# A hand-ordered kernel for a state-space scan and dilated attention: its issue order rearranged, with the load of the B matrices moved, mask constants moved on GpSimd, and four state reloads on ScalarE

## The chip, the cores and the metric

The kernel runs on one core of a Trainium2 chip. The metric is the device time of one launch in microseconds (us), the median of several runs. The five engines of the core appear under the profile's names: PE (TensorE, the matrix engine; PEld is its weight load), DVE (VectorE), ACT (ScalarE), POOL (GpSimd) and SP (SyncE, which here only issues DMA transfers; SPq in the profile). Each engine works through its own instructions in the order in which the program has them, and waits at one until what it needs is there. PSUM is the memory into which TensorE's matmuls write; VectorE and ScalarE copy ("cast") results from there into the on-chip SBUF.

## The reference

Two independent parts read a sequence of 2048 tokens with 448 channels each, and their outputs stand side by side.

```python
# part A: a diagonal state-space layer
dt = exp(log_dt); Lam_bar = exp(dt * Lam)            # complex, 448 states
B_bar = ((Lam_bar - 1.0) / Lam)[:, None] * Bmat
Bu = einsum("bld,pd->blp", x, B_bar)
for t in range(L):
    h = Lam_bar * h + Bu[:, t, :]                    # a scan over 2048 tokens
y = 2.0 * einsum("blp,dp->bld", hs, Cmat).real + x * Dskip
# part B: dilated sliding attention, 16 heads of 28, window 8, dilation 2
q, k, v = split(x @ wqkv)
logits[s, w] = q[s] . k[s - 2*w] * scale             # masked where s - 2*w < 0
o[s] = sum_w softmax(logits)[s, w] * v[s - 2*w]
out = o @ wo
return concatenate([a, b], axis=-1)
```

## The kernel before, in words

The 2048 tokens are laid out as 128 chunks of 16 consecutive tokens; "token j" below is the j-th of every chunk, so one tile of 128 rows holds token j of all chunks.

**Part B.** x of token j is loaded by a transposing DMA (L363, four tiles of 128x128 each; L359, L366 and L367 fetch the rest of the channels). TensorE projects Q and K (L478, L511 with all 128 rows; L485 two at a time with 64 rows each, for the remaining 64 channels of two tokens; for these the 64 rows are first copied to the other half of the partitions, "the dup copy"). Results leave PSUM by casts (helper L215 and L217 on ScalarE, L219 and L221 on VectorE). VectorE multiplies q with shifted k (L651, L653, L657, the products), TensorE sums each product over the 28 channels of a head in 32 columns (L669, L675, the logits) and adds the mask (L287), VectorE takes the maximum (L698), TensorE subtracts it (L702, "sub"), ScalarE exponentiates (L708), VectorE divides (L717, L719), a transposing DMA turns the weights (L724). V is projected at L750 and L757. VectorE makes the weighted sum of V, four groups g of four tokens (g = 3 and 2 first, then 1 and 0), each a run of multiplications L814 and additions L817 that ends with L826, or with L829 for g = 0. Groups 3, 2 and 1 are transposed by a DMA (L852), group 0 by TensorE (L864, tile pt_o). TensorE multiplies with wo (L880, L888, L895), and L905 sends the rows out. There are 4 staging rows for them.

**Part A.** GpSimd and VectorE work out the powers of Lam_bar from the parameters (GpSimd at L1056 to L1075; then ScalarE's exponential and sine, L1079 and L1082; then GpSimd again, L1106 to L1121; VectorE builds Gd at L1127 and the power matrices pw at L1179). TensorE forms the input matrix Bcat from Gd and B (L1163, tile ps_b, with B in the tile ra: loaded at L954 and L955, 784 KB, half of it copied to other partitions by the "ra copy"). The scan goes by seven groups m of 64 states (a complex state takes two rows): local matmuls on x (L1229, L1238), then a chain that TensorE and ScalarE hand back and forth (L1248 to L1300: casts e, eA, eB, eight small steps ubuf, S), and at its end the states of the inner tokens. There a "reload" puts an earlier result, already cast to SBUF, back into a PSUM tile, so that matmuls can add to it: either ScalarE copies it (L1304) or TensorE multiplies it with the identity (L1306). The output y is 15 matmuls per token over the states and x (L1428, L1432); L1447 sends it out from 8 staging rows. Six PSUM banks serve everything, with one double tile beside them.

**The order.** The program first collects 685 units of work (`Planner.add`), each with its possible engines. `Planner.run` then issues them in the order of the table `ORDER` (L48 on): an entry modulo 1000 is the unit's number, and an entry over 1000 picks the second of the unit's engines. Since each engine is an in-order queue, the table alone sets what stands ahead of what on every engine, SP's queue of DMA transfers among them. All units of a PSUM tile take the next free bank in that order. Where TensorE goes from one shape of tile to another (128 rows, pairs of 64 rows, logits in 32 columns) the planner reckoned with an extra cost when the table was made; the table itself is only a list.

Of the kernel before, what the change touches and what calls it, by code (L numbers as in the profile page):

```python
# [45 lines left out]
YG = ((3,), (7,), (11,), (1, 5), (9,), (0, 4), (8,), (2, 6), (10,), (12, 13), (14,), (15,))  # L46
YSPLIT = 8
ORDER = [  # L48
    1, 22, 4, 5, 2, 3, 0, 36, 7, 38, 39, 24, 1037, 26, 28, 30, 8, 6, 40, 9, 41, 42, 19, 13, 12, 49, 1043, 11,
    10, 1045, 44, 50, 62, 63, 64, 1066, 21, 220, 29, 51, 53, 65, 52, 31, 32, 54, 55, 1058, 56, 59, 1057, 60, 61,  # L50
    69, 70, 1046, 71, 72, 1073, 74, 75, 67, 87, 76, 1068, 171, 78, 79, 80, 81, 1077, 172, 82, 83, 103, 104, 88,
    1047, 105, 107, 106, 84, 86, 14, 95, 96, 85, 97, 98, 1154, 174, 15, 33, 167, 99, 90, 91, 92, 260, 168, 221,
    157, 158, 93, 373, 1094, 181, 18, 108, 109, 16, 17, 155, 48, 165, 110, 111, 1166, 100, 131, 112, 113, 182,
    175, 115, 116, 173, 183, 1114, 101, 176, 1102, 119, 134, 20, 135, 141, 137, 156, 161, 162, 159, 160, 117,
    118, 120, 163, 505, 164, 506, 507, 121, 89, 188, 508, 35, 139, 136, 123, 124, 125, 122, 127, 495, 509, 184,
    496, 179, 147, 143, 185, 126, 189, 490, 510, 511, 491, 492, 493, 494, 138, 144, 513, 514, 186, 512, 498,
    128, 499, 140, 129, 180, 177, 133, 497, 187, 132, 130, 196, 178, 500, 520, 485, 486, 206, 207, 501, 503,
    529, 487, 521, 502, 504, 522, 208, 209, 148, 145, 515, 531, 516, 517, 150, 518, 519, 149, 146, 261, 190,
    523, 142, 191, 197, 202, 203, 151, 488, 222, 223, 525, 169, 524, 192, 193, 224, 227, 225, 229, 228, 226,
    230, 194, 231, 232, 195, 233, 234, 527, 489, 262, 235, 236, 263, 237, 23, 238, 239, 210, 264, 240, 241, 266,  # L60
    242, 268, 265, 204, 25, 243, 244, 267, 270, 245, 246, 247, 269, 1250, 198, 200, 271, 272, 248, 249, 526,
    253, 1254, 211, 27, 205, 299, 199, 201, 213, 214, 530, 251, 252, 273, 274, 170, 255, 257, 300, 256, 258,
    259, 275, 276, 215, 216, 301, 302, 305, 303, 277, 306, 338, 339, 340, 278, 279, 341, 34, 280, 281, 307, 212,
    343, 342, 282, 345, 533, 534, 304, 283, 344, 347, 535, 346, 348, 308, 284, 152, 153, 536, 285, 541, 309,
    310, 349, 350, 286, 287, 311, 312, 351, 352, 289, 288, 290, 313, 353, 354, 314, 412, 355, 292, 293, 356,
    315, 316, 294, 291, 295, 317, 357, 296, 318, 319, 358, 359, 320, 617, 360, 217, 218, 297, 298, 449, 219,
    321, 322, 361, 362, 374, 363, 364, 323, 324, 375, 325, 326, 366, 365, 367, 369, 327, 368, 376, 1328, 537,
    370, 379, 380, 371, 372, 377, 329, 413, 330, 381, 414, 415, 378, 382, 383, 384, 1331, 333, 416, 417, 419,
    528, 418, 1332, 334, 385, 421, 386, 336, 420, 422, 564, 565, 423, 424, 538, 539, 540, 568, 335, 387, 388,
    337, 425, 426, 566, 450, 389, 390, 427, 428, 569, 451, 391, 429, 392, 430, 452, 393, 394, 431, 432, 453,  # L70
    567, 455, 395, 396, 433, 434, 454, 457, 456, 435, 436, 397, 398, 458, 571, 459, 542, 460, 399, 400, 437,
    443, 461, 401, 462, 463, 438, 439, 402, 464, 465, 403, 404, 466, 467, 624, 468, 1440, 441, 469, 442, 625,
    470, 445, 471, 444, 446, 447, 570, 472, 473, 629, 572, 630, 474, 634, 475, 476, 477, 1405, 637, 478, 638,
    479, 480, 482, 573, 448, 626, 574, 575, 576, 532, 631, 632, 577, 627, 407, 481, 483, 578, 579, 619, 620,
    484, 409, 628, 621, 622, 639, 635, 636, 557, 640, 641, 550, 543, 633, 544, 545, 551, 552, 553, 554, 643,
    644, 406, 642, 408, 410, 558, 559, 547, 561, 662, 665, 666, 623, 560, 546, 616, 667, 580, 671, 672, 663,
    664, 668, 669, 555, 556, 670, 645, 673, 657, 658, 659, 648, 651, 652, 411, 646, 618, 649, 650, 562, 563,
    679, 548, 549, 602, 609, 610, 611, 653, 654, 612, 603, 604, 655, 606, 656, 613, 674, 675, 614, 615, 607,
    647, 676, 586, 608, 660, 661, 605, 587, 581, 582, 591, 592, 677, 588, 589, 583, 590, 678, 593, 594, 595,
    596, 680, 681, 597, 682, 598, 599, 584, 585, 683, 684, 600, 601]  # L80
TWO_PI = 2.0 * math.pi
MAGIC = 12582912.0

# [1485 lines left out]
```

## Time and profile before

| what | us |
|---|---|
| runs: median (lowest to highest of 3) | 139.23 (138.53 to 139.27) |
| the profiled execution: its own time | 138.77 |
| its span on the profile; time outside the span | 137.1; 1.67 |
| TensorE busy in the span | 130.2 (95%) |
| VectorE busy | 121.8 (89%) |
| ScalarE busy | 94.1 (69%) |
| GpSimd busy | 20.9 (15%) |

The profiled execution lies 0.46 us below the median of the runs. TensorE ran at the full granted clock in every stretch of the span. Busy time of TensorE contains short waits: a matmul's recorded duration (0.38 us for 512 columns) is longer than its distance to the next one in a running series (0.22 us), so up to 0.16 us of waiting behind one shows as busy.

### The profile page before, as it was taken

Reading aid. Unit: us, or ns where it says so; the run is one execution under the profiler, and the core shown is the slowest. Engines: PE = TensorE matmul, PEld = TensorE weight load, DVE = VectorE, ACT = ScalarE, POOL = GpSimd, SP = SyncE. Lnnn points to the kernel's source line nnn. Section 1 sums busy time; section 2 is a strip of 40 time slices with the busy share of each in tenths; the row PEclk is TensorE's granted clock in tenths of the full one; section 3 lists DMA queues with packets and bytes.
Section 4 is the critical chain, followed back from the end, with each engine's and each line's share of the span. In section 5 each row is a group of like instructions: output and inputs, shape, how many; then the busy total and the mean of one; then the engine's idle time right before and its main releaser. Section 6 shows DMA issues by size and latency. Waiting matters only on the chain.

```text
span 137.1 us, 2829 instructions
## 1 busy us (share of the span) xinstructions
PE 130.2 (95%) x1059; PEld 66.2 (48%) x1064; DVE 121.8 (89%) x131; ACT 94.1 (69%) x209; POOL 20.9 (15%) x69
## 2 busy tenths in 40 slices
PE   7999969999999899999999999999999999999990
PEld 2533424464555363556345643455664555545750
DVE  1636789999999999999999999999999999999950
ACT  3359949899493767588789799979659332608641
POOL 7581898009100000000000000000000000000000
PEclk9999999999999999999999999999999999999999
DMA  4978953564452444478948329810074434824443
GB/s 132 270 125 206 183 89 37 107 180 87 76 115 53 88 83 108 124 217 169 144 75 163 73 45 241 196 33 2 0 134 138 133 103 91 219 61 133 135 154 114
DMA packets 41694, 16.58 MB, mean 121 GB/s; under 512 B 33685, under 2 KB 41044, under 8 KB 41681
## 3 DMA queue, kind: packets, MB, share of 16 engines
q1 hardware_dynamic: 41618, 16.40, 52.2%
q8 instruction: 8, 0.13, 0.4%
q14 instruction: 5, 0.04, 0.1%
q10 hardware_dynamic: 63, 0.01, 0.0%
HBM read 4.32 MB, written 3.67 MB: 58 GB/s over the span
## 4 chain that ended last, share of the span: by engine, by line
PE 60%; DVE 19%; SPq 10%; ACT 4%; DMA 3%; issue 2%; DVEq 0%; ACTq 0%
PE y_ps L1432 15%; DVE prods L653 7%; SPq L363 7%; PE scb L1229 6%; PE wo_ps L888 5%; PE scp L1229 5%; DVE prods L657 3%; DMA rb<-in_B_x_dram 3%; DVE pw L1179 3%; DVE prods L651 2%; PE logits L669 2%; PE wo_ps L895 2%; PE scb L1283 2%; PE scP L1229 2%; PE v_ps L757 2%
## 5 line engine op out<-in xcount | busy, mean ns | idle before, releaser
L814 DVE TENSOR_TENSOR prods<-attn,vd 128x3584 bf16<-128x3584 bf16 x12 | 23.9, 2017 | 0.0
L817 DVE TENSOR_TENSOR rb<-rb,prods 128x3584 bf16<-128x3584 bf16 x11 | 22.2, 2018 | 0.1
L653 DVE TENSOR_TENSOR prods<-qk 128x3072 bf16<-128x3072 bf16 (+1 forms) x15 | 19.2, 1323 | 0.2
L478 PE MATMUL qk_ps<-rb 128*128 128x512 bf16 x60 | 14.6, 379 | 1.3 <-DMA rb<-in_B_x_dram 1.3
L1432 PE MATMUL y_ps<-Ccat,qk 128*128 128x448 bf16 x60 | 14.5, 352 | 0.0
L215 ACT CAST qk<-wo_ps 128x448 bf16<-128x448 f32 (+1 forms) x16 | 8.3, 533 | 7.1 <-PE wo_ps L888 4.8
L215 ACT CAST vd<-v_ps 128x448 bf16<-128x448 f32 x16 | 8.3, 534 | 4.3 <-PE logits L287 2.1
L1229 PE MATMUL scb<-xaT_sb,Bcat 128*128 128x512 bf16 x42 | 11.1, 381 | 0.1
L1229 PEld LDWEIGHTS <-Bcat 128*128 128x128 bf16 x84 | 7.7, 100 | 7.1 <-issue 0.8
L217 ACT ACTIVATE qk<-qk_ps 128x512 bf16<-128x512 f32 (+1 forms) x17 | 9.8, 598 | 1.8 <-PE qk_ps L485 1.7
L1432 PE MATMUL y_ps<-Ccat,h 128*128 128x448 bf16 x45 | 11.0, 353 | 0.0
L757 PE MATMUL v_ps<-rb 128*128 128x448 bf16 x48 | 10.3, 354 | 0.0
L478 PEld LDWEIGHTS <-rb 128*128 128x128 bf16 x60 | 5.4, 97 | 8.5 <-issue 2.1
L1276 ACT CAST ubuf<-scb 128x64 bf16<-128x64 f32 x35 | 6.7, 217 | 3.8 <-PE scb L1283 1.8
L215 ACT CAST qk<-qk_ps 128x512 bf16<-128x512 f32 (+2 forms) x14 | 8.2, 587 | 1.3 <-POOL angr L1073 1.0
L657 DVE TENSOR_TENSOR prods<-qk 128x768 bf16<-128x768 bf16 (+3 forms) x18 | 9.1, 563 | 0.0
L215 ACT CAST qk<-y_ps 128x448 bf16<-128x448 f32 (+1 forms) x9 | 5.8, 678 | 4.8 <-PE y_ps L1432 4.8
L1432 PEld LDWEIGHTS <-qk 128*128 128x128 bf16 x60 | 5.9, 98 | 5.2
L814 DVE TENSOR_TENSOR rb<-attn,vd 128x3584 bf16<-128x3584 bf16 x4 | 8.1, 2024 | 0.2
L1179 DVE TENSOR_TENSOR pw<-Dm,spair 128x1920 bf16<-128x1920 bf16 x7 | 8.2, 1192 | 0.0
L1229 PE MATMUL scp<-xaT_sb,Bcat 128*128 128x512 bf16 x30 | 7.9, 382 | 0.0
L888 PE MATMUL wo_ps<-wo_p,rb 128*128 128x448 bf16 x36 | 7.8, 353 | 0.1
(200 smaller groups left out, 258.6 us busy)
## 6 DMA issues: line engine op xcount, KB each, us to landing
out_dram<-qk SPq DMA_DIRECT2D x32, 112.0 KB, 1.7
vd<-vd SPq DMA_DIRECT2D x3, 392.0 KB, 4.4
rb<-in_B_wqkv_dram SPq DMA_DIRECT2D x3, 336.0 KB, 4.2
qk<-in_A_x_dram SPq DMA_DIRECT2D x1, 448.0 KB
ra<-in_A_B_re_dram SPq DMA_DIRECT2D x1, 392.0 KB, 4.3
ra<-in_A_B_im_dram SPq DMA_DIRECT2D x1, 392.0 KB
rb<-in_A_C_re_dram SPq DMA_DIRECT2D x4, 98.0 KB, 2.8
rb<-in_A_C_im_dram SPq DMA_DIRECT2D x4, 98.0 KB, 4.3
```

The source lines that it names most:

```text
L215: nc.scalar.copy(out, in_)
L217: nc.scalar.mul(out, in_, scale)
L478: nc.tensor.matmul(out(n), lhsT=w(n, full, k), rhs=self.xT[:, j:j + 4, k, :], start=(not rfirst and k == 1), stop=(rfirst and k == KT - 1) ...
L653: V.tensor_tensor(out.rearrange("p i j k q -> p i (j k) q"), qq.unsqueeze(1).to_broadcast([NCH, 2, 4 * nk, NCH]), bass.AP(kk.tensor, kk.of ...
L657: V.tensor_tensor(jk(out[:, i, a:e]), qq, kk, op=ALU.mult)
L757: nc.tensor.matmul(box["ps"][:].rearrange("p h d -> p (h d)"), lhsT=self.xT[:, j, k, :], rhs=self.wv[:, k, :], start=False, stop=(k == KT ...
L814: V.tensor_tensor(tmp[i].rearrange("p (j d h) -> p j d h", j=8, d=DH), aa, self.vd[:, o:o + 8], op=ALU.mult)
L817: V.tensor_tensor(acc, acc, tmp[i], op=ALU.add)
L888: nc.tensor.matmul(ps[:], lhsT=self.oTd[g][:, a + kt], rhs=self.wo_p[:, 5 * e + kt, :], start=False, stop=(kt == 2), skip_group_check=True)
L1179: V.tensor_tensor(t[:], self.o["Dm"][:].rearrange("p (a b) -> p a b", b=2).unsqueeze(1).to_broadcast([NCH, 2 * NPW, 32, 2]), self.sp[:, m ...
L1229: mt(box[i], lhsT=self.Bcat[:, k, m, :], rhs=self.xk(slice(i, None, 4), k), start=(i % 2 == 0 and k == 0), stop=False, **kw)
L1432: nc.tensor.matmul(ps, lhsT=h, rhs=self.Ccat[:, m, :], start=(m == 0 and not skip), stop=(m == NM - 1), skip_group_check=True)
```

## The change

Only the table `ORDER` is another: the same 685 units, in a new order, some on their other engine. Two lines of each table as an illustration:

```diff
 ORDER = [
-    1, 22, 4, 5, 2, 3, 0, 36, 7, 38, 39, 24, 1037, 26, 28, 30, 8, 6, 40, 9, 41, 42, 19, 13, 12, 49, 1043, 11,
-    10, 1045, 44, 50, 62, 63, 64, 1066, 21, 220, 29, 51, 53, 65, 52, 31, 32, 54, 55, 1058, 56, 59, 1057, 60, 61,
+    1, 22, 4, 5, 2, 3, 0, 36, 7, 1037, 38, 39, 40, 24, 26, 28, 41, 8, 6, 9, 30, 49, 1043, 44, 50, 62, 1042, 13,
+    63, 45, 64, 1065, 51, 1052, 54, 55, 56, 21, 29, 53, 69, 70, 58, 1057, 1059, 1060, 1061, 46, 74, 1066, 71,
...
```

SP's queue near the start, as a difference; each row is one issue or a run of equal ones (`x4`), with the line, the tile written and the source:

```order
 L340 DMA rb<-in_B_wqkv_dram 128x3x448
 L342 DMA rb<-in_B_wqkv_dram 64x448
-L363 DMA_TRANSPOSE rb<-in_B_x_dram 128x4x128 x4
+L363 DMA_TRANSPOSE rb<-in_B_x_dram 128x4x128 x8
 L954 DMA ra<-in_A_B_re_dram 64x7x448
 L955 DMA ra<-in_A_B_im_dram 64x7x448
-L363 DMA_TRANSPOSE rb<-in_B_x_dram 128x4x128 x4
 L359 DMA_TRANSPOSE xb_rest<-in_B_x_dram 128x1x128
 L363 DMA_TRANSPOSE rb<-in_B_x_dram 128x4x128 x2
```

The first four transposes are x of tokens 8 to 11, the next four x of tokens 4 to 7. The two loads of B stood between them and now stand behind both.

VectorE's queue from its first work on x to Gd, before:

```order
L219 COPY rb<-rb 64x4x128
L221 TENSOR_SCALAR qk<-qk_ps 128x4x128
L219 CAST qk<-qk_ps 64x4x128
L219 CAST qk<-qk_ps 128x4x128
L219 COPY rb<-rb 64x4x128
L219 CAST qk<-qk_ps 128x4x128
L221 TENSOR_SCALAR qk<-qk_ps 128x4x128
L651 TENSOR_TENSOR prods<-qk 128x1536
L219 CAST qk<-qk_ps 128x4x128
L651 TENSOR_TENSOR prods<-qk 128x1536
L219 COPY rb<-rb 64x4x128
L219 COPY ra<-ra 128x7x64
```

Behind these stand one more product L651, Gd (L1127) and three powers (L1179). And now:

```order
L219 COPY wm<-rb 128x512
L221 TENSOR_SCALAR qk<-qk_ps 128x4x128
L219 CAST qk<-qk_ps 128x4x128 x2
L219 CAST qk<-qk_ps 64x4x126
L221 TENSOR_SCALAR qk<-qk_ps 64x512 x2
L221 TENSOR_SCALAR qk<-qk_ps 128x4x128
L219 CAST qk<-qk_ps 128x4x128 x3
L574 COPY qk<-qk 128x24
L651 TENSOR_TENSOR prods<-qk 128x1536 x2
L221 TENSOR_SCALAR qk<-qk_ps 64x512 x2
L651 TENSOR_TENSOR prods<-qk 128x1536
L1127 TENSOR_TENSOR Gd<-Dm,gs 128x896
```

Twelve casts out of PSUM (the rows with qk_ps, counting `x2` and `x3`; the first is the L221) stand ahead of Gd instead of six, the ra copy follows Gd instead of preceding it, and the dup copies of x (rb<-rb 64x4x128) have gone to ScalarE. After Gd VectorE has four such casts fewer than before. The first TensorE work on tokens 4 to 7 is now a 64-row pair (L485), which needs the dup copy; before it was a 128-row unit (L478), which doesn't.

GpSimd's queue around the second half of the parameters, as a difference (mrow and mcol are the mask constants that L287 reads):

```order
 L1074 TENSOR_SCALAR kc<-kf 128x105
 L1075 TENSOR_TENSOR angr<-angr,kc 128x105
+L272 MEMSET mrow 128x4
+L274 AFFINE_SELECT mrow<-mrow 128x2x2
+L276 MEMSET mcol 128x512
+L280 AFFINE_SELECT mcol<-mcol 128x128 x4
 L1106 TENSOR_TENSOR cs<-sh 128x210
 L1107 TENSOR_SCALAR cs<-cs 128x210
```

The masks stood behind L1121, the last step of the parameters, and now stand in the gap in which ScalarE works out the sine. The clearing of S (L1194) went the other way, from ahead of L1056 to behind L1121.

SP's queue in the last third, from the Dskip row on (L852 are the transposes of groups g = 2 and g = 1, L905 outputs of part B, L1447 of part A):

```order
L1399 DMA rb<-in_A_Dskip_dram 128x448
L905 DMA out_dram<-qk 128x448 x2
L770 DMA vd<-vd 112x1792
L771 DMA vd<-vd 15x1792
L852 DMA_TRANSPOSE rb<-rb 128x14x128 x2
L1447 DMA out_dram<-qk 128x448 x4
L905 DMA out_dram<-qk 128x448
```

Thirty of the 32 outputs now stand behind the transpose of g = 1. Before, ten outputs stood ahead of it and 22 behind.

Elsewhere the order moves in many places. Reloads by ScalarE (L1304) go from seven to four, by TensorE (L1306) from nine to twelve. Changes of tile shape on TensorE go from 51 to 58, three of the seven before the first local matmuls of the scan and four behind, where the logits of the first eight tokens come in four blocks between the scan's steps instead of two. Counting PSUM casts and copies together, VectorE has one more than before and ScalarE one fewer (its reloads aside).

## The prediction before the run

> **What bounds the kernel now.** I read the shares of the engines first, then stretches of the span, then the waits that TensorE has in them. In the first row each engine has busy us, share and instructions; in the stretches the columns are length, busy time of PE, PEld, DVE, ACT and POOL, then clock and DMA.
>
> ```profile
> PE 130.2 (95%) x1059; PEld 66.2 (48%) x1064; DVE 121.8 (89%) x131; ACT 94.1 (69%) x209; POOL 20.9 (15%) x69
> ```
>
> ```profile
> 17.26:24.00 6.74, 5.41 (x32) 2.16 (x32) 6.24 (x8) 4.94 (x10) 6.15 (x8) 1.00 0.41 63
> 24.00:52.00 28.00, 27.45 (x314) 14.21 (x313) 27.63 (x39) 20.75 (x38) 3.75 (x6) 1.00 0.46 98
> 52.00:75.00 23.00, 22.77 (x215) 11.58 (x216) 22.61 (x19) 18.26 (x52) 0.00 (x0) 1.00 0.69 143
> 75.00:109.00 34.00, 33.59 (x254) 18.11 (x256) 33.73 (x21) 27.78 (x73) 0.00 (x0) 1.00 0.42 98
> 109.00:133.66 24.66, 24.61 (x171) 13.66 (x169) 22.59 (x17) 10.85 (x21) 0.00 (x0) 1.00 0.45 132
> 133.66:137.10 3.44, 0.00 (x1) 0.00 (x0) 0.00 (x0) 0.53 (x1) 0.00 (x0) 1.00 0.35 111
> ```
>
> TensorE is 95% busy. Length less PE busy gives its idle time by stage: 1.33 from 17.26 to 24, 0.55 from 24 to 52, 0.23, 0.41 and 0.05 in the three stages of scan and output, 3.44 at the end. VectorE is as full from 24 to 109 (27.63 of 28.00, 22.61 of 23.00, 33.73 of 34.00). So a change gains only where TensorE waits, and what it adds to TensorE costs in full. The two large waits by name:
>
> ```profile
> 18.59 1.46 PE L478 MATMUL qk_ps<-rb 128*128 128x512 bf16 x6 [1.33 <-DMA rb<-in_B_x_dram]
> ...
> 45.57 0.59 PE L702 MATMUL logits<-mx,nident 128*128 128x512 bf16 x2 [0.55 <-DVE mx L698]
> ```
>
> At 18.59 TensorE has waited 1.33 for x of tokens 4 to 7; at 45.57 it has waited 0.55 for VectorE's maximum. Short waits hide as busy, since a matmul's record is longer than its distance to the next one:
>
> ```profile
> 109.08 0.38 PE L1306 MATMUL scp<-qk,ident 128*128 128x512 bf16 x1
> 109.51 0.73 PE L888 MATMUL wo_ps<-wo_p,rb 128*128 128x448 bf16 x3
> ```
>
> One reload holds 109.08 to 109.51. A running series gives 0.22 per 512 columns (step 2), so about 0.2 of the 0.43 is waiting, and no idle time shows. Counted so over all starts after 52 us (columns, shape changes and small steps allowed for), I get some 2.9 us of waits, 0.69 of them visible as idle above. That is all that the scan and the output could give back.
>
> The sum is made against the profiled execution, 138.77 us (span 137.10 and 1.67 outside it); the median of the runs is 0.46 above. A measurement of this kernel tells about 0.5%, 0.70 us, from no change: faster is below 138.53, slower above 139.93.
>
> **Step 1: B behind x of tokens 4 to 7, and what is late next.**
>
> ```profile
> 9.24 0.67 SPq L954 DMA_DIRECT2D ra<-in_A_B_re_dram  x1
> ...
> 10.37 1.42 DVE L219 CAST qk<-qk_ps 64x512 bf16<-64x512 f32 x2 [0.46 <-PE qk_ps L478]
> 10.63 5.24 SPq L363 DMA_TRANSPOSE rb<-in_B_x_dram  x4
> ...
> 18.54 0.29 DVE L219 COPY rb<-rb 64x512 bf16<-64x512 bf16 x1 [0.47 <-DMA rb<-in_B_x_dram]
> 18.86 0.64 DVE L219 COPY ra<-ra 128x448 bf16<-128x448 bf16 x1
> 19.42 0.94 DVE L651 TENSOR_TENSOR prods<-qk 128x1536 bf16<-128x1536 bf16 x1
> ...
> 20.28 0.73 DVE L1127 TENSOR_TENSOR Gd<-Dm,gs 128x896 bf16<-128x896 bf16 x1
> ...
> 22.04 0.39 PE L1163 MATMUL ps_b<-Gd,ra 128*128 128x128 bf16 x4
> ```
>
> ```profile
> 14.61 3.74 DMA rb<-in_B_x_dram
> ...
> 21.01 3.52 DVE pw L1179 x3
> ```
>
> ```profile
> out_dram<-qk SPq DMA_DIRECT2D x32, 112.0 KB, 1.7
> ...
> ra<-in_A_B_re_dram SPq DMA_DIRECT2D x1, 392.0 KB, 4.3
> ```
>
> ```profile
> DMA to landing us min/median/max: 2.8/3.9/4.2
> ```
>
> (The rows at 14.61 and 21.01 are the chain's; then come two DMA issues, with KB and us to landing, and the landing times of x.) SP's two issues for B take 10.63 - 9.24 = 1.39 us, so the four transposes now issue from 9.24 on and the last lands about 1.4 earlier, near 17.0 instead of 14.61 + 3.74 = 18.35. That takes 1.33 of waiting off. But the first TensorE work on these tokens is now a 64-row pair behind a dup copy on ScalarE (0.29 for the like copy on VectorE at 18.54, plus its place in ScalarE's queue): a rest of 0 to 0.55, I take 0.3. Ends: if transfers also land faster with no B ahead of them, nothing is left; if the order of issue hardly counts, all 1.33 stay (a rival below).
>
> Next is VectorE. Two casts take 1.42, 0.71 each. Its first two of twelve end at about 11.0 as before; ten more at 0.71, a copy of 0.22, and three products at 0.86 (19.42 to 20.28) make 11.04 + 7.1 + 0.2 + 2.6 = 21.0 for the start of Gd, against 20.28. Gd takes 0.65 to the next start, the ra copy behind it 0.64: the first ps_b matmul can start at about 22.4. TensorE has three more projections ahead of it (0.65, step 2) and a shape change (0.1): 22.04 - 1.03 + 0.75 = 21.76. New wait: 0.6 (0 if it arrives as late as before, 1.0 if the casts run slower). B itself lands around 20.2 (issue end 15.9 plus the 4.3 that this load took before) and is no limit unless over 2 us later.
>
> From Gd to the maximum VectorE's work is nearly the same, but the ra copy (0.64), a dup copy (0.3) and a fourth power (3.52 / 3 = 1.17) come in, four casts (2.84) leave, and one group of products (0.74 to the next start, below) moves behind the maximum: with Gd 0.72 later, 0.72 + 0.64 + 0.3 + 1.17 - 2.84 - 0.74 = -0.75.
>
> ```profile
> 43.56 0.82 DVE L657 TENSOR_TENSOR prods<-qk 128x256 bf16<-128x256 bf16 x3
> 44.30 1.22 DVE L698 TENSOR_REDUCE mx<-logits 128x128 bf16<-128x1024 f32 x1
> ...
> 40.65 0.50 PE L669 MATMUL logits<-prods,Zsel 128*32 128x256 bf16 x12
> 41.20 0.50 PE L669 MATMUL logits<-prods,Zsel 128*32 128x256 bf16 x12
> ...
> 41.85 0.74 PE L750 MATMUL v_ps<-rb 64*128 64x448 bf16 x6
> ```
>
> So the maximum can start at 43.55 instead of 44.30 and TensorE's sub at 44.8 instead of 45.57, ahead of TensorE's arrival at 45.02: the 0.55 goes. The logits block just before is reached sooner by TensorE than its last product by VectorE; from the same distances I estimate 0.3 to 0.6 of waiting there and take 0.45. Waits up to 52 us are thus 0.3 + 0.6 + 0.45 = 1.35 in place of 1.33 + 0.55 = 1.88: **-0.53**, between -1.88 (all gone) and +0.75 (the 1.33 and a dup copy's 0.3 stay, the Gd wait falls into them, the 0.45 comes and the 0.55 stays).
>
> **Step 2: reloads.** ScalarE's go from seven to four, TensorE's from nine to twelve.
>
> ```profile
> L1304 ACT CAST scb<-e x3: 589/590/597, 60.7 to 95.7; 128x512 f32<-128x512 bf16 x3
> ```
>
> ```profile
> L1306 PE MATMUL scb<-e,ident x2: 376/376/377, 73.2 to 94.3; 128*128 128x512 bf16 x2
> ```
>
> ```profile
> 10.16 2.14 PE L478 MATMUL qk_ps<-rb 128*128 128x512 bf16 x9
> ```
>
> The first two rows count and give min, median and max in ns. ScalarE is freed of 3 x 0.59, 1.8 us, but is not the bound. TensorE has three more matmuls of 512 columns. Recorded 0.38, they take 0.22 in a running series (in the row at 10.16, nine of them in 2.14: (2.14 - 0.38) / 8). **+0.65**; down to 0 if all three fall into waits of the chain, up to 1.1 if each is waited for.
>
> **Step 3: changes of tile shape.** Twelve 256-column logits matmuls are 0.55 apart inside a series (40.65 to 41.20); the last block before the 64-row L750 takes 0.65 (41.20 to 41.85). So a change of shape costs about 0.10, less at others: I take 0.09. Seven more: **+0.63** (0 if each falls into a wait). The Trainium skill speaks against me here: "TensorEngine Tiling (Array Packing)", Key Properties, says that changing the tiling mode drains the TensorE, and "TensorE: Matmul & The Clock Gate", Single matmul latency, gives the constant part of one matmul as about 166 ns when warm. If each change cost that in full, seven would be an estimated 1.16 instead of 0.63, and the time 140.3; the trace's 0.10 says that most of a drain is overlapped, so I leave that reading a tenth of my forecast's chance, in its slower part.
>
> **Step 4: the masks.**
>
> ```profile
> 1.08 0.29 POOL L242 TENSOR_SCALAR_AFFINE_SELECT ident<-ident 128x128 bf16<-128x128 bf16 x1
> ...
> 13.38 0.54 POOL L1106 TENSOR_TENSOR cs<-sh 128x210 f32<-128x210 f32 x1 [2.92 <-ACT sh L1082]
> ...
> 18.41 0.10 POOL L272 MEMSET mrow<- 128x4 bf16 x1
> ...
> 19.42 4.13 POOL L280 TENSOR_SCALAR_AFFINE_SELECT mcol<-mcol 128x128 bf16<-128x128 bf16 x4
> ```
>
> GpSimd idles 2.92 us before L1106, until ScalarE's sine. Here the masks stand now. At the four selects' later price (4.13, beside VectorE's two-input products) with 1.0 for mrow and the memset (18.41 to 19.42), they would overrun by 2.2; at the 0.29 of the like select at 1.08 they take 2.0 and fit. In that gap VectorE only casts, so I take the latter, 0. An overrun would delay the powers, but L1121 ended before 18.41 and Gd starts at 21.0, so the first 2 us cost nothing. The clearing of S goes behind L1121, 30 us ahead of its use. Cost 0; up to +0.3 if both overrun and start late.
>
> **Step 5: waits of scan and output.** The 0.2 at 109.08 goes, since this reload moves to ScalarE: **-0.2**. The others, 2.7, I leave as they are: with three ScalarE copies fewer they may shrink, with logits blocks between the steps and VectorE's products later they may grow; between -1.5 (over half) and +1.5.
>
> **Step 6: the end.**
>
> ```profile
> 114.29 1.57 SPq L852 DMA_TRANSPOSE rb<-rb  x1
> ...
> 117.84 0.95 SPq L1447 DMA_DIRECT2D out_dram<-qk  x2
> ...
> 126.03 2.09 DVE L829 TENSOR_TENSOR rb<-rb,prods 128x1792 bf16<-128x1792 bf16 x2
> ...
> 127.36 1.50 PE L864 MATMUL pt_o<-ident,rb 128*128 128x128 bf16 x24
> ```
>
> TensorE's transposes L864 start 0.3 after VectorE's first L829 half (126.03 + 1.04 = 127.07): both arrive together. After Gd VectorE has four casts fewer (2.84), against 0.72, 0.64 and 0.3 from step 1: it gets there 1.2 earlier. TensorE doesn't, so this cover is worth 0. On SP thirty outputs stand behind the transpose of group g = 1, which issues 1.2 earlier too, 113.1 to 114.7. Outputs go at 0.48 each (117.84: two in 0.95), so thirty could be out at 129, before the end. Part A's eight staging rows are full until the first output has landed, 114.7 + 0.4 + 1.7 = 116.8; the ninth is wanted at 117 to 118, counted back from the end over the matmuls behind it. Cost 0, with up to 1 us to spare.
>
> **Sum.** -0.53 + 0.65 + 0.63 - 0.2 = +0.55. On the profiled execution 139.3, on the median 139.78: **139.8 us**, likely 139.2 to 140.5 by steps 1 and 3 at their nearer ends.
>
> **Rivals.**
>
> *The scan's waits shrink* (B, the other side). The chain between TensorE and ScalarE stops most where ScalarE has queued work in front of a small step; 1.8 us of it goes, and twelve identity matmuls need no cast. For: a waiting step needn't show as idle, as at 109.08. Against: only 0.69 of the waits after 52 show as idle, and each reload on TensorE sits in the same chain. If half of 2.9 goes, 139.78 - 1.5 = 138.3. It decides from 1.25 on. Chance 0.20.
>
> *Outputs held by SP* (C). If g = 1's transpose comes over 1 us later than reckoned, or TensorE reaches the ninth y earlier, ScalarE stops at a staging row, banks stay taken, and TensorE stops. One to 1.5 us: 140.8 to 141.2. Against: VectorE's lead of 1.2. Chance 0.13.
>
> *x of tokens 4 to 7 no earlier* (D). If with B gone from ahead the transposes still land when they did, held by other traffic, and the dup copy comes on top, the 1.33 stay and 0.3 with them; the wait for Gd (0.6) then falls into it. 139.78 + 1.33 - 0.6 = 140.5. For: 3.74 is near the median 3.9 of all x, so B was no great brake. Against: the order of issue then still gives 1.39. Chance 0.10.
>
> *Added work falls into the waits* (E): reloads and shape changes cost half, nothing measurable is left, 139.2. Chance 0.09.
>
> My forecast keeps 0.48: 0.01 faster, 0.25 same, 0.22 slower. B gives 0.18 faster and 0.02 same, C 0.13 slower, D 0.02 same and 0.08 slower, E 0.09 same: faster 0.19, same 0.38, slower 0.43. The range from 138.2 (half of B below it) to 141.0 (half of C above) leaves out 0.17.
>
> **What the profile after would show.** Step 1: no wait for in_B_x_dram of over 0.6 near 17 us, a new one at ps_b (L1163) near 22 for Gd or ra, no wait at L702. Step 2: twelve L1306 matmuls, PE busy 131 or more. Step 4: mcol selects near 0.3 in a gap before 13.4, and L1106 no later than 15. Step 6: the outputs' first issue behind L852 at 114.5, none of TensorE's idle time put down to a staging row. I am wrong if the idle and hidden waits after 52 us change by over 1 us either way, if ps_b waits over 1.2 us, or if TensorE stops behind y between 112 and 120.

## The result, and the profile after

| kernel | median, us | ratio to before (95% interval) |
|---|---|---|
| before | 139.06 (138.53 to 139.27, 5 runs) | |
| changed | 140.11 (140.04 to 140.32, 5 runs) | 1.0086 (1.0060 to 1.0113) |
| changed, a second time | 140.40 (140.13 to 140.76, 11 runs) | 1.0079 (1.0053 to 1.0105) |

The change makes the kernel 1.05 us slower by the medians. Here and below the medians are of all executions, while the ratios leave out five that lie far off or in a slower state (two of the kernel before, one each of the run with the two copies moved, of the three moves, and of these with one reload), which moves no median by more than 0.06 us. The profiled execution after took 140.11 us (span 138.40), 1.34 more than the one before. Stretches of the kernel after, cut at the same times as before's (length, then busy us of PE, PEld, DVE, ACT, POOL, clock, DMA share, GB/s):

```profile
17.26:24.00 6.74, 6.19 (x36) 2.57 (x36) 6.68 (x9) 6.01 (x12) 1.28 (x3) 1.00 1.13 136
24.00:52.00 28.00, 27.48 (x307) 13.65 (x305) 27.79 (x32) 20.35 (x38) 3.90 (x6) 1.00 0.48 98
52.00:75.00 23.00, 22.83 (x214) 11.05 (x216) 22.90 (x23) 15.77 (x43) 0.00 (x0) 1.00 0.60 133
75.00:109.00 34.00, 33.49 (x256) 18.38 (x257) 33.76 (x22) 26.52 (x73) 0.00 (x0) 1.00 0.49 97
133.66:138.40 4.74, 1.31 (x7) 0.49 (x5) 0.62 (x1) 0.53 (x1) 0.00 (x0) 1.00 0.35 110
```

TensorE's idle time from 17.26 to 24 is 6.74 - 6.19 = 0.55 where it was 1.33; from 24 to 52 it is 0.52 (0.55 before), and in the scan 0.17 and 0.51 (0.23 and 0.41). TensorE waits no more than before and yet ends later, for it has more to do. The waits by what ended them (us in total, times, longest):

```profile
PE ps_b L1163 <- DVE Gd L1127: 0.5, 1, 0.5
PE qk_ps L478 <- DMA rb<-in_B_wqkv_dram: 0.4, 1, 0.4
PE logits L702 <- DVE mx L698: 0.3, 1, 0.3
PE scb L1283 <- ACT ubuf L1276: 0.3, 1, 0.3
```

The wait for x of tokens 4 to 7 is gone, and Gd is waited for in its place, as forecast. The wait for wqkv lies at the very start (near 6 us) and changes from execution to execution: the first projection starts at 5.95 before and at 6.14 here, at up to 7.00 in the runs below. VectorE, GpSimd and TensorE around Gd and behind it, from the timeline after (start, us, engine):

```profile
11.27 1.25 POOL L280 TENSOR_SCALAR_AFFINE_SELECT mcol<-mcol 128x128 bf16<-128x128 bf16 x4
...
21.48 0.62 DVE L1127 TENSOR_TENSOR Gd<-Dm,gs 128x896 bf16<-128x896 bf16 x1
22.13 0.29 DVE L219 COPY ra<-ra 128x448 bf16<-128x448 bf16 x1
...
22.17 0.54 PE L1163 MATMUL ps_b<-Gd,ra 128*128 128x128 bf16 x4 [0.55 <-DVE Gd L1127]
...
26.01 1.15 DVE L1179 TENSOR_TENSOR pw<-Dm,spair 128x1920 bf16<-128x1920 bf16 x1
27.19 0.99 DVE L219 COPY rb<-rb 64x512 bf16<-64x512 bf16 x1
27.20 2.96 POOL L775 MEMSET vd<- 1x896 f32 x4 [8.66 <-DVE pw L1179]
28.21 1.16 DVE L1179 TENSOR_TENSOR pw<-Dm,spair 128x1920 bf16<-128x1920 bf16 x1
29.38 0.82 DVE L576 COPY qk<-qk 64x8 bf16<-64x8 bf16 x1
...
45.68 0.59 PE L702 MATMUL logits<-mx,nident 128*128 128x512 bf16 x2 [0.30 <-DVE mx L698]
```

The four mask selects now take 1.25 instead of 4.13, and the ra copy, no longer beside the memset of mcol, 0.29 instead of 0.64. But while GpSimd clears vd (27.20 to 30.16), VectorE's dup copy takes 0.99 where it took 0.29, and a copy of 64x8 elements 0.82 where 0.18 is its usual time: 1.3 us of VectorE that I had not reckoned with. The power of 1.16 between them is no longer than the one ahead of the clearing, 1.15. The reloads, and the end:

```profile
L1306 PE MATMUL scb<-e,ident x5: 378/379/403, 73.8 to 96.7; 128*128 128x512 bf16 x5
L1306 PE MATMUL scp<-h,ident x4: 379/384/404, 62.3 to 84.4; 128*128 128x512 bf16 x4
...
L1306 PE MATMUL scP<-qk,ident x2: 378/378/379, 95.6 to 95.8; 128*128 128x512 bf16 x2
```

```profile
113.64 1.54 SPq L852 DMA_TRANSPOSE rb<-rb  x1
115.27 2.52 SPq L1447 DMA_DIRECT2D out_dram<-qk  x4
...
125.38 2.09 DVE L829 TENSOR_TENSOR rb<-rb,prods 128x1792 bf16<-128x1792 bf16 x2
...
128.11 1.50 PE L864 MATMUL pt_o<-ident,rb 128*128 128x128 bf16 x24
```

Eleven of the twelve reload matmuls have a record. VectorE's last additions start at 125.38, 0.65 sooner than before, TensorE's transposes L864 0.75 later: VectorE has a lead at the end and it is worth nothing. SP's outputs start at 115.27 and no wait of TensorE is put down to them.

To see where 1.3 us went, I took the distance from each of TensorE's matmuls to the next and split it in three: what its columns take in a running series (0.216 us for 512; matmuls of the narrow shapes that run side by side share it), what a change of tile shape takes, and the rest. Changes of shape cost 0.093 to 0.105 in the medians of all kinds, into the narrow shapes and back alike, in both kernels.

| from the first to the last start of a matmul, us | before | after | difference |
|---|---|---|---|
| columns of the recorded matmuls | 117.58 | 118.23 | +0.65 |
| changes of shape | 51: 5.07 | 58: 5.75 | +0.68 |
| the rest (waits; five missing records in each) | 9.81 | 9.80 | -0.01 |
| all | 132.46 | 133.77 | +1.31 |

Up to 52 us the rest is 4.77 before and 4.76 after, behind it 5.05 and 5.03. (The prediction's 2.9 behind 52 us had the small steps of the scan taken off; the rest here contains them.) In this accounting the added work is the loss, and the waits were exchanged, not removed. What leaving out a part of that work would give is another question, which the runs below answer.

Two distances on TensorE are of use for them: from the first projection (L478) to the first 64-row local matmul of the scan (L1238), which leaves out when the first loads came, and from there to the last matmul. The second repeats well: 80.52, 80.52 and 80.53 in the profiled executions of the kernel before, of it with B's loads alone moved and of it with the three moves, all in the same order behind that point; 81.31, 81.30 and 81.30 in those of the changed kernel, of its second time and of it with B's loads put back.

### The profile page after: what moved, and what is told of

Its sections match the earlier page's. It is cut to its first block, busy times and chain, and to the rows that moved or that the text cites. A ratio compares the mean times of both kernels' runs of the same rounds, so it can differ in the third digit from the quotient of the medians.

```text
span 138.4 us, 2838 instructions
## 1 busy us (share of the span) xinstructions
PE 132.0 (95%) x1062; PEld 66.1 (48%) x1067; DVE 123.7 (89%) x132; ACT 91.3 (66%) x205; POOL 17.7 (13%) x69
## 4 chain that ended last, share of the span: by engine, by line
PE 66%; DVE 23%; DMA 3%; issue 3%; ACT 2%; SPq 1%; ACTq 0%; DVEq 0%
PE y_ps L1432 15%; DVE prods L653 7%; PE scb L1229 6%; PE wo_ps L888 5%; PE scp L1229 5%; DVE prods L651 3%; DMA rb<-in_B_wqkv_dram 3%; PE qk_ps L478 3%; DVE prods L657 3%; DVE qk L221 2%; PE logits L669 2%; PE scb L1283 2%; DVE qk L219 2%; DVE pw L1179 2%; PE wo_ps L895 2%
## 5 line engine op out<-in xcount | busy, mean ns | idle before, releaser
L478 PE MATMUL qk_ps<-rb 128*128 128x512 bf16 x60 | 14.6, 380 | 0.4 <-DMA rb<-in_B_wqkv_dram 0.4
L478 PEld LDWEIGHTS <-rb 128*128 128x128 bf16 x60 | 5.5, 98 | 7.2 <-DMA rb<-in_B_wqkv_dram 1.1
L217 ACT ACTIVATE qk<-qk_ps 128x512 bf16<-128x512 f32 (+1 forms) x14 | 8.1, 598 | 1.4 <-PE qk_ps L511 0.9
L888 PE MATMUL wo_ps<-wo_p,rb 128*128 128x448 bf16 x36 | 8.3, 353 | 0.0
L1179 DVE TENSOR_TENSOR pw<-Dm,spair 128x1920 bf16<-128x1920 bf16 x7 | 8.0, 1153 | 0.1
```

The costliest lines, as they stand in the source:

```text
L217: nc.scalar.mul(out, in_, scale)
L478: nc.tensor.matmul(out(n), lhsT=w(n, full, k), rhs=self.xT[:, j:j + 4, k, :], start=(not rfirst and k == 1), stop=(rfirst and k == KT - 1) ...
L888: nc.tensor.matmul(ps[:], lhsT=self.oTd[g][:, a + kt], rhs=self.wo_p[:, 5 * e + kt, :], start=False, stop=(kt == 2), skip_group_check=True)
L1179: V.tensor_tensor(t[:], self.o["Dm"][:].rearrange("p (a b) -> p a b", b=2).unsqueeze(1).to_broadcast([NCH, 2 * NPW, 32, 2]), self.sp[:, m ...
```

## The experiments

All are edits of the table alone, and none leaves work out. The kernel before ran beside each (medians 138.92 to 139.03), and the ratios are to it. Theory T at the start: the loss is the three reload matmuls and the seven shape changes, and the early gain was eaten by VectorE.

**Halves.** First the new order up to the scan and the old one behind it, then the reverse:

```diff
-ORDER = old
+ORDER = new[:240] + [u for u in old if u not in new[:240]]     # early_new; units compared modulo 1000
+ORDER = old[:232] + [u for u in new if u not in old[:232]]     # late_new; likewise
```

> The first 240 of 685 units in the new order (up to just before the first local matmuls of the scan, with their new engines), the rest in the old order with the old engines: nine reloads on TensorE and 56 changes of tile shape, against 9 and 51 before. Theory T (the loss is three matmuls for reloads, 0.65, and seven changes of shape, 0.68, while the early waits are only exchanged, 1.33 at x for as much elsewhere): five shape changes more than before, about +0.5, 139.5 us. Rival E (the early half carries the whole loss, because VectorE reaches its powers and the maximum late): +1.0, 140.1. Rival L (the early half is a gain of 0.5, as forecast, and the late half loses it): 138.6.

> The first 232 units in the old order, the rest in the new order with its engines: twelve reloads on TensorE and 57 changes of shape. Theory T: +0.65 for reloads and +0.57 for six shape changes, +1.2, 140.3 us. Rival E (all loss early): no change, 139.1. Rival L (late half loses 1.5): 140.6. If waits of scan and output had shrunk under the new late order, less than 139.8.

Measured: 142.11 us, ratio 1.0222 (1.0199 to 1.0245), and 141.90 us, 1.0217 (1.0193 to 1.0240). Each half alone loses over two and a half times what both lose together; all theories missed. TensorE's waits at the seam, of the first half new and then of the second half new:

```profile
54.02 0.51 PE L669 MATMUL logits<-prods,Zsel 128*32 128x256 bf16 x12 [0.89 <-DVE prods L653]
54.76 0.29 PE L675 MATMUL logits<-prods,Zsel 128*32 128x256 bf16 x4 [0.23 <-DVE prods L657]
56.57 0.51 PE L669 MATMUL logits<-prods,Zsel 128*32 128x256 bf16 x12 [0.65 <-DVE prods L657]
```

```profile
51.91 0.51 PE L669 MATMUL logits<-prods,Zsel 128*32 128x256 bf16 x12 [1.16 <-DVE prods L653]
```

Logits wait 0.89, 0.23 and 0.65, or 1.16, for products that VectorE makes in another sequence in the other half. These waits belong to the seam (they make up 1.8 of the 3.2 us and 1.2 of the 3.0; the rest was not followed), so the two runs don't tell where the change loses; they say that each half of such an order is fitted to the other.

**B's loads alone, on the kernel before.**

```diff
 L363 DMA_TRANSPOSE rb<-in_B_x_dram 128x4x128 x4    # x of tokens 8 to 11
-L954, L955 DMA ra<-in_A_B_re_dram, in_A_B_im_dram
 L363 DMA_TRANSPOSE rb<-in_B_x_dram 128x4x128 x4    # x of tokens 4 to 7
+L954, L955 DMA ra<-in_A_B_re_dram, in_A_B_im_dram
```

> The kernel before with only the two loads of B moved behind x of tokens 4 to 7. Theory T: x comes 1.4 earlier and TensorE's wait of 1.33 goes, but VectorE's copy of B to the other partitions, which stands ahead of Gd, now waits for B until about 20.3, Gd starts near 21.8 instead of 20.28, TensorE waits about 2 us for it, and VectorE is 1.4 later at the maximum: +0.7 to +1.4, 139.8 to 140.5 us. Rival X (the wait of 1.33 is simply taken off): 137.8. Rival D (x lands no earlier): the wait stays, and the late B comes on top, 140.5 with a wait for x of over 1 us in the profile.

140.26 us, 1.0093 (1.0075 to 1.0111): theory T, in time and place.

```profile
PE ps_b L1163 <- DVE Gd L1127: 1.7, 1, 1.7
...
PE logits L702 <- DVE mx L698: 0.6, 1, 0.6
```

The wait for x is gone and 1.7 us of waiting for Gd are there, because the ra copy stands ahead of Gd on VectorE and waits for B. The ra copy's move behind Gd is thus no detail of the change but what makes B's move possible.

**B's loads put back, in the changed kernel**, with the changed kernel beside it on the same chip:

```diff
+L954, L955 DMA ra<-in_A_B_re_dram, in_A_B_im_dram
 L363 DMA_TRANSPOSE rb<-in_B_x_dram 128x4x128 x4    # x of tokens 4 to 7
-L954, L955 DMA ra<-in_A_B_re_dram, in_A_B_im_dram
```

> The changed kernel itself, as the reference for the run that undoes one move of it. Both theories: 1.006 to 1.011 of the kernel before. If B's landing is a second limit at the first ps_b matmul (it was waited for 0.9 in two variants of this kernel), its profile shows a wait there of 0.5 to 0.9.

> The changed kernel with the loads of B put back ahead of x of tokens 4 to 7, all else kept. Theory T (in the new order x of tokens 4 to 7 is what starts everything up to the maximum): TensorE waits about 1.3 at the first 64-row pair and no longer at ps_b (0.55 or 0.9), VectorE's early casts come later by the same: +0.5 to +1.0 against the changed kernel. Rival B (B's late landing costs as much at ps_b as x's early landing gives): 0.0.

140.69 us, 1.0099 (1.0066 to 1.0133), against 140.40, 1.0079 (1.0053 to 1.0105): 0.3 us, with intervals that overlap widely, so the times don't decide between the two. The profiles do, for rival B: where theory T has a wait of 1.3, 0.44 are seen. Gd, the first pairs on tokens 4 to 7 and ps_b, of the changed kernel and then with B put back:

```profile
17.39 0.39 PE L485 MATMUL qk_ps<-rb 64*128 64x512 bf16 x2
...
21.62 0.62 DVE L1127 TENSOR_TENSOR Gd<-Dm,gs 128x896 bf16<-128x896 bf16 x1
...
22.47 0.54 PE L1163 MATMUL ps_b<-Gd,ra 128*128 128x128 bf16 x4 [0.70 <-DMA ra<-in_A_B_im_dram]
```

```profile
17.45 0.39 PE L485 MATMUL qk_ps<-rb 64*128 64x512 bf16 x2
18.08 0.37 PE L485 MATMUL qk_ps<-rb,wm 64*128 64x512 bf16 x1 [0.24 <-DMA rb<-in_B_x_dram]
18.65 0.37 PE L485 MATMUL qk_ps<-rb 64*128 64x512 bf16 x1 [0.20 <-ACT rb L215]
...
21.68 0.62 DVE L1127 TENSOR_TENSOR Gd<-Dm,gs 128x896 bf16<-128x896 bf16 x1
...
22.63 0.39 PE L1163 MATMUL ps_b<-Gd,ra 128*128 128x128 bf16 x4
```

With B first TensorE loses 0.24 for x and 0.20 for its dup copy, and then finds Gd and B ready; with B last it waits 0.70 for B (in this execution B lands last, in the first profile Gd came last). VectorE starts Gd at 21.6 or 21.7 either way: its twelve casts fill it from 11 us on, whichever comes first. From the first projection to L1238 the two take 47.34 and 47.25, from there to the end both 81.30: on the traces B's move is worth nothing in the new order, and by the medians 0.3 us that can't be told from nothing.

**The two slowed copies.** The dup copy back to ScalarE, the 64x8 copy ahead of the powers:

```diff
+L576 COPY qk<-qk 64x8
 L1179 TENSOR_TENSOR pw<-Dm,spair 128x1920 x2
-L219 COPY rb<-rb 64x4x128                           # to ScalarE
 L1179 TENSOR_TENSOR pw<-Dm,spair 128x1920
-L576 COPY qk<-qk 64x8
 L1179 TENSOR_TENSOR pw<-Dm,spair 128x1920
```

> The changed kernel with two copies on VectorE out of the way of GpSimd's four clearings of vd (27.2 to 30.2 us in the profile after): the dup copy that took 0.99 goes to ScalarE, the copy at L576 that took 0.82 moves ahead of the four powers. Theory T (these two were slow because GpSimd was clearing at the same time: alone they take 0.30 and 0.18, so VectorE lost 1.3 us before the maximum): VectorE reaches the maximum 1.3 to 2 us sooner, the waits of 0.30 at the subtraction, 0.3 behind the 64-row pair at 27.7 and 0.16 inside the logits block go, -0.5 to -0.7, 139.5 us. Rival C (the copies were long for a reason of their own, a full queue or late data): VectorE waits there for something else, the maximum stays, no change, 140.1.

140.42 us, 1.0100 (1.0077 to 1.0122): not faster. Theory T was right on the copies and wrong on the time:

```profile
25.72 0.18 DVE L576 COPY qk<-qk 64x8 bf16<-64x8 bf16 x1
25.93 4.37 DVE L1179 TENSOR_TENSOR pw<-Dm,spair 128x1920 bf16<-128x1920 bf16 x4
...
33.25 1.76 DVE L653 TENSOR_TENSOR prods<-qk 128x3072 bf16<-128x3072 bf16 x1 [0.68 <-ACT qk L215]
...
29.27 0.37 PE L485 MATMUL qk_ps<-rb 64*128 64x512 bf16 x1 [0.51 <-ACT rb L215]
...
45.92 0.59 PE L702 MATMUL logits<-mx,nident 128*128 128x512 bf16 x2
```

The copy takes 0.18 again and the four powers 1.09 each, beside GpSimd's clearing from 27.86 on. TensorE no longer waits at L702. But now TensorE waits 0.51 for the dup copy on ScalarE, and VectorE, which is sooner by then, waits 0.68 for a cast of ScalarE, the engine that was given the dup copy. What VectorE lost was one of several limits that lie within half a microsecond of each other. This execution also began its projections 0.8 later (6.95 for 6.14). Counted from there it reaches L1238 in 46.62, where the changed kernel takes 47.17: some of what T forecast may be there, but with one profiled execution the edit and the late start can't be told apart.

**Reloads.** Only the engine of five reloads, in both orders:

```diff
-    250, 328, 332, 440, 1406        # new order: four by ScalarE in all
+    1250, 1328, 1332, 1440, 406     # as before: seven (reload7); and the reverse in the old order (before_reload4)
```

> The changed kernel with the engines of the reloads as before (seven on ScalarE, nine on TensorE), the order kept. Theory T (each matmul more on TensorE costs its 0.22, ScalarE's 0.59 are hidden): -0.65, 139.5 us. Rival S (in the new order ScalarE's queue is what the small steps of the scan wait for, which is why reloads left it): the 0.65 come back as waits at L1279 to L1300, 140.1 or more.

> The kernel before with the engines of the reloads as in the changed one (four on ScalarE, twelve on TensorE), the order kept. Theory T: +0.65, 139.6 us. Rival S (the matmuls fall into waits, or ScalarE's freed 1.8 us shorten as many): 139.0 or less.

In the old order, three more on TensorE: 139.42 us, 1.0032 (1.0012 to 1.0051), that is +0.44 (0.17 to 0.71), an interval that holds T's 0.65 and shuts out rival S. On the traces it is 81.01 for 80.52 from L1238 to the last matmul, +0.49, so that about a quarter of the matmuls' time falls into waits. In the new order, three more on ScalarE: 143.56 us, 1.0321 (1.0297 to 1.0344), 3 us slower than the changed kernel. T is refuted there, and rival S understated. TensorE's waits and one of the places, with ScalarE's queue ahead of it, with seven reloads on ScalarE:

```profile
PE scb L1299 <- ACT scb L1304: 2.9, 3, 1.6
```

```profile
63.26 0.48 ACT L1296 CAST h<-scb 128x384 bf16<-128x384 f32 x1
63.64 0.60 ACT L1304 CAST scp<-h 128x512 f32<-128x512 bf16 x1
64.16 0.22 ACT L1276 CAST ubuf<-scb 128x64 bf16<-128x64 f32 x1
64.26 0.60 ACT L1304 CAST scb<-e 128x512 f32<-128x512 bf16 x1
...
64.92 0.22 PE L1299 MATMUL scb<-S,pw 128*128 128x128 bf16 x1 [1.04 <-ACT scb L1304]
```

ScalarE has the second reload only after an eviction, another reload and a small step; the next matmul of the chain stands right behind the reload and waits 1.04. With the reload on TensorE the same matmul has no wait, in the changed kernel:

```profile
63.63 0.22 PE L1299 MATMUL scb<-S,pw 128*128 128x128 bf16 x1
```

From L1238 on this execution takes 84.44 for 81.31. The new order has no room for a ScalarE reload at these places: the three matmuls are part of it.

**Shape changes.** Three of the four logits blocks between the scan's steps put together:

```diff
-    ... 197 ... 203 ... 193 ...
+    ... 197, 203, 193 ...           # three units of L669 and L675 in a row
```

> The changed kernel with three of the four blocks of logits of the first eight tokens, which it has between steps of the scan, put together as one (54 changes of tile shape instead of 58). Theory T (each change costs 0.09 to 0.10): -0.38, 139.7 us. Rival H (the blocks stood where TensorE would have waited for ScalarE, so the changes were hidden): the waits of the scan grow by as much, 140.1. Rival P (VectorE must now keep three products until the block has read them, and stops): 140.3 or more.

140.87 us, 1.0130 (1.0105 to 1.0154), where the changed kernel has 1.0079 (1.0053 to 1.0105): not faster, and rather slower, with 54 shape changes for 58. From L1238 to the last matmul it is 81.63 for 81.31, so 0.32 of it belong to the edit where T has -0.38; before L1238 nothing was changed, and there this execution waited 0.9 for B. Rival H, and a wait of VectorE, though not the one that rival P has:

```profile
61.45 0.27 PE L1265 MATMUL scb<-eA,pw 128*128 128x256 bf16 x1 [0.29 <-ACT eA L1262]
...
64.29 1.23 DVE L698 TENSOR_REDUCE mx<-logits 128x128 bf16<-128x1024 f32 x1 [0.33 <-PE logits L287]
```

The scan waits 0.29 for ScalarE where a logits block had stood, and the maximum starts at 64.29, after 0.33 of waiting for the last logits (P has VectorE stopping for room for its products, and no such wait is there); in the changed kernel it started at 63.54 at once (0.43 of the difference is that this execution reached the scan later). The accounting's 0.68 for shape changes is what they take; it isn't what leaving them out gives.

**What can be kept of the change.** Three moves that add nothing to TensorE, on the kernel before; then the last reload to ScalarE, which idles there; then one cast of Bcat to ScalarE:

```diff
-L954, L955 ... ahead of x of tokens 4 to 7
+L954, L955 ... behind x of tokens 4 to 7
-L219 COPY ra<-ra ahead of L1127 Gd
+L219 COPY ra<-ra behind L1127 Gd
-L272 to L280 (masks) behind L1121
+L272 to L280 (masks) ahead of L1106
+1406 instead of 406                 # trio_406: the last reload by ScalarE
+166 instead of 1166                 # trio_casts: and one cast of Bcat by ScalarE
```

> The kernel before with three moves only, none of which adds work to TensorE: B behind x of tokens 4 to 7, VectorE's ra copy behind Gd, the mask constants in GpSimd's gap. Theory T (the new early order is right, what it lost is extra casts on VectorE, shape changes and reloads): the wait of 1.33 for x goes, Gd comes at about 20.0 with the ra copy behind it until 20.6, TensorE waits at ps_b not over 0.3, VectorE is 0.5 to 0.8 sooner at the maximum, while TensorE's wait there grows from 0.55 to about 1: -0.5 to -0.9, 138.2 to 138.5 us. Rival V (VectorE sets the early part in any order): the whole 1.33 comes back at ps_b and at the maximum, 139.0.

> The three moves on the kernel before (B behind x of tokens 4 to 7, ra copy behind Gd, masks in the gap), and one reload, the last one, from TensorE to ScalarE, which idles 1.8 us there. Theory T: the three moves give 0.25 as measured, the reload 0.22 of matmul and 0.2 of waiting at 109.08: 138.4 to 138.6 us, ratio 0.995 to 0.997. Rival S (TensorE waits for ScalarE's reload as it did when three were put back into the new order): no gain over the three moves, ratio 0.998 or more.

> The same, and one cast of Bcat (needed only 20 us later) from VectorE to ScalarE. Theory T (VectorE sets the maximum, for which TensorE waits 0.6): VectorE is 0.7 sooner there, the wait goes, -0.4 to -0.6 more, 137.9 to 138.2 us. Rival Q (ScalarE is full from 22 to 35 us and passes the 0.59 on to the banks that TensorE needs): no gain or a loss, 138.5 or more.

| | us | ratio to before |
|---|---|---|
| three moves | 138.78 | 0.9982 (0.9966 to 0.9999) |
| and the last reload on ScalarE | 138.47 | 0.9949 (0.9923 to 0.9975) |
| and one cast on ScalarE | 138.29 | 0.9947 (0.9928 to 0.9966) |

The three moves alone give 0.25 us (0 to 0.5), less than T and more than rival V had: a gain near what can be told. On the traces it is larger: from the first projection to L1238 the three versions take 45.96, 45.96 and 45.98, where the old order takes 46.84 (46.83 in before_reload4, which is the same to that point). But their profiled executions began the projections at 7.00, 6.80 and 6.46, the kernel before at 5.95, and why they began later is open. The reload brings 0.3 to 0.5 more by the medians, as T had (the two versions ran on different chips, and their intervals overlap), and 0.23 on the traces from L1238 on (80.30 for 80.53), the matmul's own time; a reload may go to ScalarE where ScalarE idles. The last step gives nothing more that can be told. Waits of TensorE, of the three moves and of the last version:

```profile
PE logits L702 <- DVE mx L698: 0.6, 1, 0.6
PE qk_ps L478 <- ACT qk L217: 0.3, 1, 0.3
```

```profile
PE qk_ps L478 <- DMA rb<-in_B_x_dram: 0.5, 1, 0.5
PE ps_b L1163 <- DVE qk L219: 0.3, 1, 0.3
```

With the three moves nothing waits for x or at ps_b; the maximum is waited for 0.6 as before. In the last version this wait is gone, but 0.5 for a later x transfer (at 25.95, not for tokens 4 to 7) and 0.3 at ps_b are there, and the time stays. The versions with the reload beat both kernels.

## Why the prediction was right, and where it was short

The time (140.11 for 139.8), its direction and its likely range held. The forecast was +0.55; the medians moved +1.05, and the profiled executions +1.34. That 140.11 lies so near 139.8 is in part luck: the median before to which the prediction added its sum, 139.23 of three runs, lies 0.17 above the median of five. By the prediction's own line (139.93) the kernel is slower, which it gave 0.43; its central value, 139.78, lay below that line. The mechanism was right in the added work and wrong in the early waits, which were to pay for part of it. By the steps:

- **Step 2, reloads.** +0.65 in columns, as forecast. What they cost in time was measured in the old order only: 0.44 (0.17 to 0.71), 0.49 on the traces.
- **Step 3, shape changes.** 58 for 51, 0.099 each, +0.68 for 0.63. The reading that each would cost the 166 ns which the Trainium skill ("TensorE: Matmul & The Clock Gate", Single matmul latency) gives as a matmul's constant part is not borne out: no kind of change costs more than 0.105 in the median.
- **Step 5.** Waits behind 52 us: 5.05 and 5.03, for -0.2 forecast. From the first 64-row local matmuls of the scan (L1238, at 52.79 and 53.31) to the last matmul the kernel takes 80.52 before and 81.31 after. The new order has 0.24 us more of its work done at that point (eight sums of the softmax, 0.46, less two groups of logits matmuls, 0.22), so +1.03 on equal work: the reloads' 0.65 and four shape changes in full.
- **Step 1 is the step that was mis-sized.** Up to L1238 it is +0.52, or +0.28 on equal work; without three shape changes (0.30) the waits come to 0 where I had -0.53, and 0.19 of that is the later start of the first projection. The single waits came out well: 0.55 at ps_b for 0.6, none for x for 0.3. The first of them is luck in part: Gd started at 21.48 for 21.0, and the ra copy, which the prediction has in front of the first ps_b matmul, wasn't waited for (that matmul starts at 22.17, the copy ends at 22.42). Wrong was the 0.55 at the maximum, which I took off in full and of which 0.30 stayed, and 0.3 more behind the 64-row pair at 27.71, which I had not seen: VectorE lost 1.3 us in two copies beside GpSimd's clearing. I had followed GpSimd's masks and not its next work. Putting B back in the new order cost nothing that can be told: the 1.33 were never to be had there, since that order fills VectorE with casts, and Gd starts at 21.6 or 21.7 either way. Nor was the 1.33 a fixed price in the old order: in before_reload4, which began its projections at 6.50, the wait was 0.94, and the way from the first projection to L1238 still took 46.83 (46.84 before). That the two copies are the cause of the whole rest is not shown: without them the time was no better.
- **Step 4.** Masks at no cost: right, 0.35 each. They gave something, too: the ra copy went from 0.64 to 0.29.
- **Step 6.** Cost 0: right. SP's outputs began at 115.27 for 114.7 and nothing waited for them (rival C). VectorE's lead at the end is 0.65 for 1.2, worth 0.
- **Rivals D and E** were not seen: nothing waited for x of tokens 4 to 7, and the table's rest did not shrink while 1.33 of work was added. **Rival B** fell: the scan's waits did not shrink. In its reasoning ScalarE's freed time shortens the chain; the run with seven ScalarE reloads shows why it doesn't: the new order had already spent that time by putting the matmul that needs a reload right behind it.

## What to carry to other kernels

Where TensorE is 95% busy, count first what a new order adds to TensorE (matmuls, changes of tile shape), then ask of each wait removed which engine is late next, and add up that engine's work to that point, its slowed instructions too. An order, its engine choices and its groupings are fitted to each other: halves of it, or the reloads' engines turned back, lose more (2 to 3%) than the whole change (0.9%), so a part is judged by adding it to the old order, with the moves that it needs (B's move alone lost 0.9% too), rather than by taking it out of the new one. And read a stretch that begins behind the first loads beside the total: they come at another time in each execution (the first projection between 5.95 and 7.00 here). Look for moves that cost the bounding engine nothing: three such and one reload out of this change gave 0.5% where the whole lost 0.9%.

## What the runs showed of the hardware that I had not expected

VectorE's copies within SBUF take longer while GpSimd clears memory: 0.99 for 0.29 and 0.82 for 0.18, whereas a product of two SBUF operands beside the same clearing takes 1.16 for 1.15. GpSimd's selects, which read, took 1.03 each in the mean beside VectorE's products, 0.35 beside casts out of PSUM, and 0.35 with VectorE idle (in the run with B's loads alone moved, from 19.93 on). The Trainium skill, "SBUF — State Buffer", Who interferes with whom, says the same: copies in a two-port mode contend with any GpSimd instruction, those with two SBUF inputs only with one that reads. The trace agrees on all three, though no view shows in which mode a copy ran. That the wait is for the whole of the other's instruction, as the page has it, fits roughly: 0.29 and 0.18, each with one clearing of 0.74 (a quarter of 2.96), make 1.03 and 0.92 for 0.99 and 0.82; in early_new the second copy met a shorter clearing, of 0.47, and took 0.54 for 0.65. Three cases don't prove it.
